# Attention scores as three float32r products, and a shared last step of values for two pairs of heads

## The chip, the cores and the metric

The kernel runs on one core of a Trainium2 chip. The metric is the time of one execution on the device, in microseconds. Engines are named TensorE (PE, with its weight loads as PEld), ScalarE (ACT), VectorE (DVE), GpSimd (POOL) and SyncE (SP, which issues the transfers).

## The reference

Sigmoid attention over 4 batches, 12 heads, 448 tokens and 64 dimensions, then two layers of a feed-forward block on 1792 tokens, all of it in float32:

```python
scores = scale * np.matmul(q, k.transpose(0, 1, 3, 2)) - np.log(S)
attn = 1.0 / (1.0 + np.exp(-scores))
x = np.matmul(attn, v)            # then tokens by 768 columns
h = x @ w_in;  x = (np.maximum(h, 0) ** 2) @ w_out
h = x @ w_in2; out = (np.maximum(h, 0) + alpha * np.minimum(h, 0)) @ w_out2
```

The feed-forward weights come as float64.

## The kernel before

Two stages follow one another. The attention stage works through 24 units; a unit is one batch and two heads. The feed-forward stage then takes the rest of the time; the change leaves its code as it is. All instructions stand in the queues in the order in which the program writes them: TensorE, ScalarE, VectorE, GpSimd and SyncE each work through their own queue.

A unit's 448 keys are 3 x 128 and 64 left over (R = 3, MAIN = 384, REM = 64). Its steps:

- fetch(u), L122: eight transfers on SyncE: q and k for two heads (L135), their last 64 rows (L137), v (L132) and its last 64 rows into vrem (L137). NAT = 3 buffers of each.
- turn(u), L139: seven transposes on TensorE bring q and k to 64 dimensions on the partitions, one head in partitions 0 to 63, the other in 64 to 127, into two accumulator banks; VectorE copies the 896 columns to qkt (L150).
- scores(u, j), L152: for step j of four, the keys of that step (128 columns of weights) against all 448 queries, for each head in its half of the rows (L159), in float32, which gives two matmul instructions for a product; then one sigmoid on ScalarE over both heads, 2 x 448 columns (L161). Two buffers of two banks. In the last step the weights are the 64 left keys and 64 others, so half of the sigmoid's output is not used.
- values(u, j), L164: the step's sigmoids against v, in float32, each head into its half of the columns of one bank (L172), added over the four steps. In the last step the spare 64 rows of vrem are zero (cleared once at the start, L188).
- finish(u), L176, after the last step: the bank goes to the feed-forward stage's x in two parts, a high part in float32r by ScalarE (L184) and the rest by VectorE (L185). The 448 tokens of a batch fall into one tile of x (batch 0) or two (batches 1 to 3; 64 + 384, 128 + 320, 64 + 384 columns), and each piece has its own pair of instructions.

The loop (L193) writes for unit u: scores(u, 0) and (u, 1); values(u-1, 2) and (u-1, 3) with the finish of u-1; fetch(u+2); turn(u+1); scores(u, 2) and (u, 3); values(u, 0) and (u, 1). Weights for the next stage are fetched beside it: load (L62) brings 768 KB through three buffers, assemble (L74) turns float64 into float32 with one instruction on ScalarE (L82) and three on VectorE (L83 to L85), split (L87) makes the high part on ScalarE (L95) and the rest on GpSimd (L96), and then issues the load for three items later, which needs the buffer that GpSimd has just read. Loads 0 to 2 are issued in units 2, 4, 6; assemble(i) stands in unit 8 + 2i, split(i) in unit 9 + 2i, for i from 0 to 5.

In the feed-forward stage each product is three float32r products, high by high, high by low and low by high (L227, L260).

Of the kernel before, what the change touches and what calls it, by code (L numbers as in the profile page):

```python
# [9 lines left out]
F32 = mybir.dt.float32  # L10
F32R = mybir.dt.float32r
I32 = mybir.dt.int32
I64 = mybir.dt.int64
AF = mybir.ActivationFunctionType
ALU = mybir.AluOpType
P = 128
# [3 lines left out]
def fused_kernel(ctx: ExitStack, tc: tile.TileContext, q, k, v, w1i, w1o, w2i, w2o, alpha, out):  # L20
# [12 lines left out]
    nc = tc.nc  # L33
    B, H, S, D = q.shape
# [4 lines left out]
    R = S // P  # L39
    MAIN = R * P  # L40
    REM = S - MAIN
# [3 lines left out]
    SCALE = 1.0 / math.sqrt(D)  # L45
# [9 lines left out]
    bias = const.tile([P, 1], F32, name="bias")  # L55
# [6 lines left out]
    def load(i):  # L62
        if i >= len(items):
            return
        layer, inward, f = items[i]
        w = ((w1i, w1o), (w2i, w2o))[layer][0 if inward else 1]
        raws[i] = wpool.tile([P, DM, 2], I32, tag="raw", name=f"raw{i}", bufs=3)
        d = raws[i].rearrange("p m t -> p (m t)").bitcast(I64)
        if inward:
            nc.sync.dma_start(out=d.rearrange("p (c f) -> p c f", c=NC), in_=w[:, f * P:(f + 1) * P].rearrange("(c p) f -> p c f", p=P))  # L70
        else:
            nc.sync.dma_start(out=d, in_=w[f * P:(f + 1) * P, :])

    def assemble(i):  # L74

        if i >= len(items):
            return  # L80
        low, high = raws[i][:, :, 0], raws[i][:, :, 1]
        nc.scalar.activation(high.bitcast(F32), high.bitcast(F32), AF.Copy, scale=2.0 ** -112)  # L82
        nc.vector.tensor_scalar(out=low, in0=low, scalar1=29, scalar2=None, op0=ALU.logical_shift_right)  # L83
        nc.vector.scalar_tensor_tensor(out=low, in0=high, scalar=3, in1=low, op0=ALU.logical_shift_left, op1=ALU.bitwise_or)  # L84
        nc.vector.scalar_tensor_tensor(out=low, in0=high, scalar=-2 ** 31, in1=low, op0=ALU.bitwise_and, op1=ALU.bitwise_or)  # L85

    def split(i):  # L87
        if i >= len(items):
            return
        layer, inward, f = items[i]  # L90
        w = raws.pop(i)[:, :, 0].bitcast(F32)
        tag = "wi" if inward else "wo"
        hi = wpool.tile([P, DM], F32R, tag=tag + "h", name=f"wh{i}", bufs=3)
        lo = wpool.tile([P, DM], F32R, tag=tag + "l", name=f"wl{i}", bufs=3)
        nc.scalar.activation(hi, w, AF.Copy)  # L95
        nc.gpsimd.tensor_sub(lo, w, hi)  # L96
        ready[items[i]] = (hi, lo)
        load(i + 3)
# [4 lines left out]
    def x_tiles(layer, t, c):  # L103
        n = TILES[t][1]
        if (layer, t, c) not in x:
            x[layer, t, c] = tuple(xpool.tile([P, n], F32R, tag=f"x{part}{t}", name=f"x{part}{layer}_{t}_{c}", bufs=NC) for part in "hl")
        return x[layer, t, c]

    with tc.manual_schedule():
# [6 lines left out]
        with tc.tile_pool(name="apool", bufs=1) as apool, tc.tile_pool(name="apsum", bufs=1, space=bass.MemoryType.PSUM) as psum:  # L116
            units = [(b, c) for b in range(B) for c in range(H // 2)]
            NAT = 3
            nats, qks, vals, qkt, sig, avs = {}, {}, {}, {}, {}, {}
            vrem = [apool.tile([P, 2, D], F32, name=f"vrem{i}") for i in range(NAT)]  # L120

            def fetch(u):  # L122
                if u >= len(units):
                    return
                b, c = units[u]
                hs = slice(2 * c, 2 * c + 2)
                nats[u] = apool.tile([P, 2, R, 2, D], F32, tag="nat", name=f"nat{u}", bufs=NAT)
                vals[u] = apool.tile([P, 2, R, D], F32, tag="v", name=f"v{u}", bufs=NAT)
                qks[u] = apool.tile([P, 2, D], F32, tag="qk", name=f"qk{u}", bufs=NAT)
                for j, src in enumerate((q, k, v)):  # L130
                    if j == 2:
                        nc.sync.dma_start(out=vals[u], in_=src[b, hs, :MAIN, :].rearrange("h (p r) d -> p h r d", r=R))  # L132
                    else:
                        for h in range(2):
                            nc.sync.dma_start(out=nats[u][:, j, :, h, :], in_=src[b, 2 * c + h, :MAIN, :].rearrange("(p r) d -> p r d", r=R))  # L135
                    last = (qks[u][:REM], qks[u][REM:], vrem[u % NAT][:REM])[j]
                    nc.sync.dma_start(out=last, in_=src[b, hs, MAIN:, :].rearrange("h p d -> p h d"))  # L137

            def turn(u):  # L139

                if u >= len(units):
                    return
                ps = psum.tile([P, 1024], F32, tag="tp", name=f"tp{u}", bufs=1)
                for r in range(R):
                    nc.tensor.transpose(ps[:, r * P:(r + 1) * P], nats[u][:, 0, r].rearrange("p h d -> p (h d)"), eye)  # L145
                nc.tensor.transpose(ps[:, MAIN:MAIN + P], qks.pop(u).rearrange("p h d -> p (h d)"), eye)  # L146
                for r in range(R):
                    nc.tensor.transpose(ps[:, 512 + r * P:512 + (r + 1) * P], nats[u][:, 1, r].rearrange("p h d -> p (h d)"), eye)  # L148
                qkt[u] = apool.tile([P, 2 * S], F32, tag="qkt", name=f"qkt{u}", bufs=2)
                nc.vector.tensor_copy(qkt[u], ps[:, :2 * S])  # L150

            def scores(u, j):  # L152

                t = qkt[u]
                at = S if j == R else 512 + j * P
                ps = psum.tile([P, 2, 512], F32, tag="sc", name=f"sc{u}_{j}", bufs=2)
                for h in range(2):
                    rows = slice(h * D, (h + 1) * D)
                    nc.tensor.matmul(ps[:, h, :S], t[rows, at:at + P], t[rows, :S], start=True, stop=True)  # L159
                a = apool.tile([P, 2, S], F32, tag="a", name=f"a{u}_{j}", bufs=6)  # L160
                nc.scalar.activation(a, ps[:, :, :S], AF.Sigmoid, bias=bias, scale=SCALE)  # L161
                sig[u, j] = a

            def values(u, j):  # L164
                if u < 0:
                    return
                if j == 0:
                    avs[u] = psum.tile([P, 512], F32, tag="av", name=f"av{u}", bufs=2)
                a = sig.pop((u, j))
                for h in range(2):  # L170
                    w = vrem[u % NAT][:, h, :] if j == R else vals[u][:, h, j, :]
                    nc.tensor.matmul(avs[u][h * D:(h + 1) * D, :S], w, a[:, h, :], start=(j == 0), stop=(j == R))  # L172
                if j == R:
                    finish(u)

            def finish(u):  # L176
                b, c = units[u]
                ps = avs.pop(u)
                for t, (first, n) in enumerate(TILES):
                    lo, hi = max(first, b * S), min(first + n, (b + 1) * S)  # L180
                    if lo < hi:
                        xh, xl = (p[:, lo - first:hi - first] for p in x_tiles(0, t, c))
                        part = ps[:, lo - b * S:hi - b * S]
                        nc.scalar.activation(xh, part, AF.Copy)  # L184
                        nc.vector.tensor_sub(xl, part, xh)  # L185

            for i in range(NAT):
                nc.gpsimd.memset(vrem[i][REM:], 0.0)  # L188
            fetch(0)
            fetch(1)  # L190
            nc.sync.dma_start(out=al, in_=alpha.rearrange("(f p) -> p f", p=P))
            turn(0)
            for u in range(len(units)):  # L193
                scores(u, 0)
                scores(u, 1)
                values(u - 1, 2)
                values(u - 1, R)
                fetch(u + 2)
                turn(u + 1)
                scores(u, 2)  # L200
                scores(u, R)
                values(u, 0)
                values(u, 1)

                if u in (2, 4, 6):
                    load(u // 2 - 1)
                if u >= 8 and u % 2 == 0 and u // 2 - 4 < 6:
                    assemble(u // 2 - 4)
                if u >= 8 and u % 2 == 1 and u // 2 - 4 < 6:
                    split(u // 2 - 4)  # L210
            values(len(units) - 1, 2)
            values(len(units) - 1, R)


        gpool = ctx.enter_context(tc.tile_pool(name="gpool", bufs=1, reuse_waits="tile"))
# [127 lines left out]
```

## Time and profile before

| | us |
|---|---|
| median of 3 runs | 1135.44 (1134.73 to 1136.49) |
| the profiled execution | 1135.57 |
| its span, first to last instruction | 1133.8 |
| TensorE busy | 1115.6 (98%) |
| VectorE busy | 642.5 (57%) |
| ScalarE busy | 362.2 (32%) |
| first matmul of the feed-forward stage | at 193.53 |

The shares are means over both stages. The attention stage is a sixth of the span. In the views, a time such as 121.38 is in us from the start of the span; a matmul's duration holds its way through the array, so consecutive matmuls overlap, and the distance of their starts tells what one costs.

### The profile page before, as it was taken

How to read it: one execution, taken by the hardware profiler on the slowest of the kernel's cores; microseconds unless marked ns; L12 is line 12 of the kernel's file. 1: busy time of each engine (PE TensorE's matmuls, PEld its weight loads, DVE VectorE, ACT ScalarE, POOL GpSimd, SP SyncE). 2: the span in 40 equal slices, each digit the busy share in tenths (PEclk: the TensorE clock that was granted, in tenths of full speed). 3: DMA queues.
4: the chain of work that ended last, by engine and by line, in shares of the span. 5: the costliest groups of instructions: out<-in, count | busy, mean ns of one | idle time of the engine just before them, and what ended most of it. 6: DMA issues, size and time to landing. Idle time of an engine off the chain costs nothing.

```text
span 1133.8 us, 14165 instructions
## 1 busy us (share of the span) xinstructions
PE 1115.6 (98%) x5736; PEld 933.6 (82%) x5736; DVE 642.5 (57%) x943; ACT 362.2 (32%) x536; POOL 153.2 (14%) x97
## 2 busy tenths in 40 slices
PE   7999999999999999999999999999999999999998
PEld 3444344898989898989898999898989898989998
DVE  1233431335666665656666674567676767767554
ACT  4567765443222222322224543312121212121110
POOL 0001110011111111110103560101010202011000
PEclk9999999999999999999999999999999999999999
DMA  5645551011121202020202020202020211110014
GB/s 110 154 113 140 145 139 39 1 56 56 44 68 32 80 29 84 28 84 29 84 28 84 28 84 29 84 27 80 8 84 28 80 33 56 57 56 28 1 56 139
DMA packets 89265, 73.28 MB, mean 65 GB/s; under 512 B 52592, under 2 KB 83312, under 8 KB 89200
## 3 DMA queue, kind: packets, MB, share of 16 engines
q1 hardware_dynamic: 89200, 72.38, 22.2%
q8 instruction: 45, 0.74, 0.3%
q14 instruction: 20, 0.16, 0.0%
HBM read 66.85 MB, written 5.51 MB: 64 GB/s over the span
## 4 chain that ended last, share of the span: by engine, by line
PE 93%; DVE 4%; ACT 2%; SPq 0%; issue 0%; DMA 0%; ACTq 0%
PE h L227 39%; PE o L260 38%; PE sc L159 7%; PE av L172 7%; DVE raw L84 1%; PE tp L145 1%; PE tp L148 1%; DVE r L237 1%; DVE g L238 1%; ACT gh L239 1%; DVE raw L85 1%; ACT raw L82 1%; ACT wh L95 0%; DVE acc L265 0%; DVE gl L240 0%; PE tp L146 0%
## 5 line engine op out<-in xcount | busy, mean ns | idle before, releaser
L227 PE MATMUL h<-xh,wl 128*128 128x512 f32 (+1 forms) x768 | 278.5, 363 | 0.0
L227 PE MATMUL h<-xl,wh 128*128 128x512 f32 (+1 forms) x768 | 278.3, 362 | 0.0
L227 PE MATMUL h<-xh,wh 128*128 128x512 f32 (+1 forms) x768 | 277.9, 362 | 0.0
L96 POOL TENSOR_TENSOR wl<-raw,wh 128x768 fp32r<-128x768 f32 x64 | 122.3, 1911 | 908.1 <-ACT wh L95 850.6
L265 DVE TENSOR_TENSOR acc<-o,acc 128x384 f32<-128x384 f32 (+1 forms) x364 | 200.0, 584 | 76.8 <-PE o L260 75.3
L260 PE MATMUL o<-wh,gh 128*128 128x384 f32 x448 | 150.6, 336 | 6.5 <-DVE acc L265 6.2
L227 PEld LDWEIGHTS h<-xh,wh 128*128 128x128 f32 x768 | 144.2, 188 | 15.6 <-issue 0.7
L227 PEld LDWEIGHTS h<-xl,wh 128*128 128x128 f32 x768 | 144.1, 188 | 15.1
L227 PEld LDWEIGHTS h<-xh,wl 128*128 128x128 f32 x768 | 144.1, 188 | 15.1
L260 PE MATMUL o<-wl,gh 128*128 128x384 f32 x448 | 149.9, 335 | 0.0
L260 PE MATMUL o<-wh,gl 128*128 128x384 f32 x448 | 149.8, 334 | 0.0
L260 PE MATMUL o<-gh,wl 128*128 128x512 f32 (+1 forms) x384 | 139.1, 362 | 0.0
L260 PE MATMUL o<-gl,wh 128*128 128x512 f32 (+1 forms) x384 | 139.0, 362 | 0.0
L260 PE MATMUL o<-gh,wh 128*128 128x512 f32 (+1 forms) x384 | 138.9, 362 | 0.0
L239 ACT ACTIVATE gh<-g 128x512 fp32r<-128x512 f32 (+1 forms) x64 | 37.1, 579 | 284.4 <-DVE g L238 284.4
L240 DVE TENSOR_TENSOR gl<-g,gh 128x512 fp32r<-128x512 f32 (+1 forms) x128 | 93.0, 727 | 52.3 <-ACT gh L239 45.4
L95 ACT ACTIVATE wh<-raw 128x768 fp32r<-128x768 f32 x64 | 57.3, 896 | 175.1 <-DVE raw L85 129.2
L161 ACT ACTIVATE a<-sc,bias 128x896 f32<-128x896 f32 x96 | 91.8, 1005 | 57.4 <-PE sc L159 57.4
L234 DVE SCALAR_TENSOR_TENSOR g<-h,r 128x512 f32<-128x512 f32 (+1 forms) x64 | 39.9, 623 | 113.9 <-ACT r L233 113.9
L84 DVE SCALAR_TENSOR_TENSOR raw<-raw 128x768 int32<-128x768 int32 x64 | 81.1, 1267 | 39.6 <-ACT raw L82 35.4
L233 ACT ACTIVATE r<-h 128x512 f32<-128x512 f32 (+1 forms) x64 | 34.8, 544 | 186.4 <-PE h L227 185.7
L260 PEld LDWEIGHTS o<-wh,gh 128*128 128x128 f32 x448 | 84.1, 188 | 9.4 <-DVE acc L265 8.1
(39 smaller groups left out, 1094.6 us busy)
## 6 DMA issues: line engine op xcount, KB each, us to landing
raw<-in_moe_w_in_dram SPq DMA_DIRECT2D x32, 768.0 KB, 4.8
raw<-in_moe_w_out_dram SPq DMA_DIRECT2D x32, 768.0 KB, 4.3
nat<-in_q_dram SPq DMA_DIRECT2D x48, 96.0 KB, 2.9
nat<-in_k_dram SPq DMA_DIRECT2D x48, 96.0 KB, 2.9
v<-in_v_dram SPq DMA_DIRECT2D x24, 192.0 KB, 2.7
out_dram<-acc SPq DMA_DIRECT2D x16, 192.0 KB, 2.7
out_dram<-acc SPq DMA_DIRECT2D x6, 384.0 KB, 2.3
qk<-in_q_dram SPq DMA_DIRECT2D x24, 32.0 KB, 2.5
```

The costliest lines, as they stand in the source:

```text
L84: nc.vector.scalar_tensor_tensor(out=low, in0=high, scalar=3, in1=low, op0=ALU.logical_shift_left, op1=ALU.bitwise_or)
L95: nc.scalar.activation(hi, w, AF.Copy)
L96: nc.gpsimd.tensor_sub(lo, w, hi)
L159: nc.tensor.matmul(ps[:, h, :S], t[rows, at:at + P], t[rows, :S], start=True, stop=True)
L161: nc.scalar.activation(a, ps[:, :, :S], AF.Sigmoid, bias=bias, scale=SCALE)
L172: nc.tensor.matmul(avs[u][h * D:(h + 1) * D, :S], w, a[:, h, :], start=(j == 0), stop=(j == R))
L227: nc.tensor.matmul(ps[:, :n], wp[:, c * P:(c + 1) * P], xp, start=(c == 0 and i == 0), stop=(c == NC - 1 and i == 2))
L234: nc.vector.scalar_tensor_tensor(out=gt, in0=ps[:, :n], scalar=0.0, in1=r, op0=ALU.max, op1=ALU.mult)
L239: nc.scalar.activation(gh, gt, AF.Copy)
L240: nc.vector.tensor_sub(gl, gt, gh)
L260: nc.tensor.matmul(ps[:, :size], *ops, start=(i == 0), stop=(i == len(turns) - 1))
L265: nc.vector.tensor_add(part, ps[:, :size], part)
```

## The change

- turn makes two tiles of q and k in float32r instead of one in float32: a high part, by VectorE's copy, and a low part, by a VectorE subtraction from the same accumulators.
- scores makes three float32r products per head and step (high by high, high by low, low by high), added in the accumulators, where one float32 product stood.
- The last 64 keys of a unit go to partitions 0 to 63 for even units and 64 to 127 for odd ones (the 128 columns of weights begin 64 earlier for these), and the sigmoid takes these 64 partitions alone, into a tile that the two units of a pair share. The last 64 rows of v are laid out in the same way.
- The last step of values is done for both units of a pair at one place, last_values: four products of 64 rows by 64 columns. Both finishes follow there.
- The loop goes over pairs of units (u, w = u + 1). It has the same steps; values(u, 3) is gone from the middle, fetch(u+3) and turn(u+2) stand after values(u, 2). assemble(i) and split(i-1) both stand at the end of a pair's steps, so that each split, and the load behind it, comes one unit later.
- v has four buffers, and the clearing of vrem is gone.

```diff
--- before.py
+++ after.py
@@ -116,8 +116,7 @@
         with tc.tile_pool(name="apool", bufs=1) as apool, tc.tile_pool(name="apsum", bufs=1, space=bass.MemoryType.PSUM) as psum:
             units = [(b, c) for b in range(B) for c in range(H // 2)]
             NAT = 3
-            nats, qks, vals, qkt, sig, avs = {}, {}, {}, {}, {}, {}
-            vrem = [apool.tile([P, 2, D], F32, name=f"vrem{i}") for i in range(NAT)]
+            nats, qks, vals, vrems, parts, sig, avs = {}, {}, {}, {}, {}, {}, {}
 
             def fetch(u):
                 if u >= len(units):
@@ -125,16 +124,21 @@
                 b, c = units[u]
                 hs = slice(2 * c, 2 * c + 2)
                 nats[u] = apool.tile([P, 2, R, 2, D], F32, tag="nat", name=f"nat{u}", bufs=NAT)
-                vals[u] = apool.tile([P, 2, R, D], F32, tag="v", name=f"v{u}", bufs=NAT)
+                vals[u] = apool.tile([P, 2, R, D], F32, tag="v", name=f"v{u}", bufs=NAT + 1)
                 qks[u] = apool.tile([P, 2, D], F32, tag="qk", name=f"qk{u}", bufs=NAT)
+                if u % 2 == 0:
+                    vrems[u // 2] = apool.tile([P, 2, D], F32, tag="vrem", name=f"vrem{u}", bufs=3)
                 for j, src in enumerate((q, k, v)):
                     if j == 2:
                         nc.sync.dma_start(out=vals[u], in_=src[b, hs, :MAIN, :].rearrange("h (p r) d -> p h r d", r=R))
                     else:
                         for h in range(2):
                             nc.sync.dma_start(out=nats[u][:, j, :, h, :], in_=src[b, 2 * c + h, :MAIN, :].rearrange("(p r) d -> p r d", r=R))
-                    last = (qks[u][:REM], qks[u][REM:], vrem[u % NAT][:REM])[j]
+                    last = (qks[u][:REM], qks[u][REM:], vrems[u // 2][half(u)])[j]
                     nc.sync.dma_start(out=last, in_=src[b, hs, MAIN:, :].rearrange("h p d -> p h d"))
+
+            def half(u):
+                return slice(u % 2 * REM, (u % 2 + 1) * REM)
 
             def turn(u):
 
@@ -146,32 +150,48 @@
                 nc.tensor.transpose(ps[:, MAIN:MAIN + P], qks.pop(u).rearrange("p h d -> p (h d)"), eye)
                 for r in range(R):
                     nc.tensor.transpose(ps[:, 512 + r * P:512 + (r + 1) * P], nats[u][:, 1, r].rearrange("p h d -> p (h d)"), eye)
-                qkt[u] = apool.tile([P, 2 * S], F32, tag="qkt", name=f"qkt{u}", bufs=2)
-                nc.vector.tensor_copy(qkt[u], ps[:, :2 * S])
+                parts[u] = [apool.tile([P, 2 * S], F32R, tag=f"qk{part}", name=f"qk{part}{u}", bufs=2) for part in "hl"]
+                nc.vector.tensor_copy(parts[u][0], ps[:, :2 * S])
+                nc.vector.tensor_sub(parts[u][1], ps[:, :2 * S], parts[u][0])
 
             def scores(u, j):
 
-                t = qkt[u]
-                at = S if j == R else 512 + j * P
+                hi, lo = parts[u]
+                at = 512 + j * P if j < R else S - u % 2 * REM
                 ps = psum.tile([P, 2, 512], F32, tag="sc", name=f"sc{u}_{j}", bufs=2)
-                for h in range(2):
-                    rows = slice(h * D, (h + 1) * D)
-                    nc.tensor.matmul(ps[:, h, :S], t[rows, at:at + P], t[rows, :S], start=True, stop=True)
-                a = apool.tile([P, 2, S], F32, tag="a", name=f"a{u}_{j}", bufs=6)
-                nc.scalar.activation(a, ps[:, :, :S], AF.Sigmoid, bias=bias, scale=SCALE)
-                sig[u, j] = a
+                for i, (kt, qt) in enumerate(((hi, hi), (hi, lo), (lo, hi))):
+                    for h in range(2):
+                        rows = slice(h * D, (h + 1) * D)
+                        nc.tensor.matmul(ps[:, h, :S], kt[rows, at:at + P], qt[rows, :S], start=(i == 0), stop=(i == 2))
+                if j < R:
+                    a = sig[u, j] = apool.tile([P, 2, S], F32, tag="a", name=f"a{u}_{j}", bufs=6)
+                    at = slice(0, P)
+                else:
+                    if u % 2 == 0:
+                        sig[u // 2] = apool.tile([P, 2, S], F32, tag="ar", name=f"ar{u}", bufs=2)
+                    a = sig[u // 2]
+                    at = half(u)
+                nc.scalar.activation(a[at], ps[at, :, :S], AF.Sigmoid, bias=bias[at], scale=SCALE)
 
             def values(u, j):
                 if u < 0:
                     return
                 if j == 0:
                     avs[u] = psum.tile([P, 512], F32, tag="av", name=f"av{u}", bufs=2)
-                a = sig.pop((u, j))
+                a, w = sig.pop((u, j)), vals[u]
                 for h in range(2):
-                    w = vrem[u % NAT][:, h, :] if j == R else vals[u][:, h, j, :]
-                    nc.tensor.matmul(avs[u][h * D:(h + 1) * D, :S], w, a[:, h, :], start=(j == 0), stop=(j == R))
-                if j == R:
-                    finish(u)
+                    nc.tensor.matmul(avs[u][h * D:(h + 1) * D, :S], w[:, h, j, :], a[:, h, :], start=(j == 0), stop=False)
+
+            def last_values(d):
+
+                if d < 0:
+                    return
+                a, w = sig.pop(d), vrems.pop(d)
+                for h in range(2):
+                    for u in (2 * d, 2 * d + 1):
+                        nc.tensor.matmul(avs[u][h * D:(h + 1) * D, :S], w[half(u), h, :], a[half(u), h, :], start=False, stop=True)
+                finish(2 * d)
+                finish(2 * d + 1)
 
             def finish(u):
                 b, c = units[u]
@@ -184,32 +204,41 @@
                         nc.scalar.activation(xh, part, AF.Copy)
                         nc.vector.tensor_sub(xl, part, xh)
 
-            for i in range(NAT):
-                nc.gpsimd.memset(vrem[i][REM:], 0.0)
             fetch(0)
             fetch(1)
             nc.sync.dma_start(out=al, in_=alpha.rearrange("(f p) -> p f", p=P))
             turn(0)
-            for u in range(len(units)):
+            for u in range(0, len(units), 2):
+                w = u + 1
                 scores(u, 0)
                 scores(u, 1)
                 values(u - 1, 2)
-                values(u - 1, R)
+                last_values(u // 2 - 1)
                 fetch(u + 2)
-                turn(u + 1)
+                turn(w)
                 scores(u, 2)
                 scores(u, R)
                 values(u, 0)
                 values(u, 1)
-
+                scores(w, 0)
+                scores(w, 1)
+                values(u, 2)
+                fetch(u + 3)
+                turn(u + 2)
+                scores(w, 2)
+                scores(w, R)
+                values(w, 0)
+                values(w, 1)
+
+                i = u // 2 - 4
                 if u in (2, 4, 6):
                     load(u // 2 - 1)
-                if u >= 8 and u % 2 == 0 and u // 2 - 4 < 6:
-                    assemble(u // 2 - 4)
-                if u >= 8 and u % 2 == 1 and u // 2 - 4 < 6:
-                    split(u // 2 - 4)
+                if 0 <= i < 6:
+                    assemble(i)
+                if 0 < i < 7:
+                    split(i - 1)
             values(len(units) - 1, 2)
-            values(len(units) - 1, R)
+            last_values(len(units) // 2 - 1)
 
 
         gpool = ctx.enter_context(tc.tile_pool(name="gpool", bufs=1, reuse_waits="tile"))
```

## Rows read from the trace of the kernel before

**Rows 1.** The table of stretches, 120 to 150 us.

```profile
core 0: us, PE busy (x) PEld busy (x) DVE busy (x) ACT busy (x) POOL busy (x), PEclk, DMA share, GB/s
120.00:150.00 30.00, 30.00 (x156) 12.37 (x156) 11.90 (x18) 21.07 (x28) 3.70 (x2) 1.00 0.59 145
```

**Rows 2.** The chain in order of time, one unit: start us, us, what.

```profile
120.06 0.48 PE tp L145 x3
...
120.97 1.70 PE sc L159 x8
122.68 1.65 PE av L172 x8
...
127.69 0.48 PE tp L145 x3
128.17 0.11 PE tp L146
128.28 0.33 PE tp L148 x3
```

**Rows 3.** The timeline of TensorE, a group of scores: start us, us, engine line operation.

```profile
120.90 0.30 PEld L159 LDWEIGHTS sc<-qkt 64*128 64x128 f32 x4 [0.17 <-issue]
121.38 0.54 PE L159 MATMUL sc<-qkt 64*128 64x448 f32 x2
121.39 0.19 PEld L159 LDWEIGHTS sc<-qkt 64*128 64x128 f32 x2 [0.18 <-ACT xh L184]
121.76 0.54 PE L159 MATMUL sc<-qkt 64*128 64x448 f32 x2
```

**Rows 4.** The timeline of TensorE in the feed-forward stage, float32r products.

```profile
302.74 0.33 PE L260 MATMUL o<-gh,wl 128*128 128x384 f32 x1
302.92 0.39 PE L227 MATMUL h<-xh,wh 128*128 128x512 f32 x1
303.15 0.40 PE L227 MATMUL h<-xl,wh 128*128 128x512 f32 x1
```

**Rows 5.** The timeline of TensorE at the end of the attention stage.

```profile
190.37 2.48 PE L172 MATMUL av<-a,v 128*64 128x448 f32 x12
...
193.53 0.50 PE L227 MATMUL h<-xh,wh 128*128 128x512 f32 x1
```

**Rows 6.** The timeline of ScalarE and VectorE, one finish and what follows.

```profile
120.11 0.28 ACT L184 ACTIVATE xh<-av 128x128 fp32r<-128x128 f32 x1 [0.44 <-PE av L172]
120.42 0.29 DVE L185 TENSOR_TENSOR xl<-av,xh 128x128 fp32r<-128x128 f32 x1 [5.34 <-ACT xh L184]
120.74 0.44 ACT L184 ACTIVATE xh<-av 128x320 fp32r<-128x320 f32 x1 [0.36 <-DVE xl L185]
121.21 0.49 DVE L185 TENSOR_TENSOR xl<-av,xh 128x320 fp32r<-128x320 f32 x1 [0.50 <-ACT xh L184]
121.62 1.08 DVE L150 COPY qkt<-tp 128x896 f32<-128x896 f32 x1
122.03 1.91 ACT L161 ACTIVATE a<-sc,bias 128x896 f32<-128x896 f32 x2 [0.86 <-PE sc L159]
```

**Rows 7.** Groups by line and shape, 0 to 215 us: busy, mean ns | idle before.

```profile
L185 DVE TENSOR_TENSOR xl<-av,xh 128x448 fp32r<-128x448 f32 x6 | 3.8, 625 | 36.5 <-ACT xh L184 36.5
L184 ACT ACTIVATE xh<-av 128x448 fp32r<-128x448 f32 x6 | 3.3, 543 | 2.7 <-PE av L172 2.7
```

**Rows 8.** The timeline around a split and the load behind it (SPq: SyncE).

```profile
116.20 0.91 ACT L95 ACTIVATE wh<-raw 128x768 fp32r<-128x768 f32 x1
116.63 1.77 PE L159 MATMUL sc<-qkt 64*128 64x448 f32 x8
117.18 1.85 POOL L96 TENSOR_TENSOR wl<-raw,wh 128x768 fp32r<-128x768 f32 x1 [13.42 <-ACT wh L95]
119.06 0.35 SPq L72 DMA_DIRECT2D raw<-in_moe_w_out_dram  x1
...
123.43 0.62 SPq L137 DMA_DIRECT2D qk<-in_k_dram  x1
```

**Rows 9.** The view of line 137, 103 to 175 us: its transfers.

```profile
DMA to landing us min/median/max: 2.2/2.6/4.7
```

## The prediction

> **What bounds the kernel now.** I read the table of stretches first: from 120 to 150 us, in the middle of the attention stage, TensorE is busy all the time at a granted clock of 1.00 (2.4 GHz), ScalarE 70% and VectorE 40% [rows 1]. Then the chain in order of time for one unit (two heads) of that stage: it is TensorE alone, 7.63 us from one turn to the next (127.69 - 120.06), made of a turn of 0.92 (0.48 + 0.11 + 0.33), two groups of scores of 1.70 and two groups of values of 1.65 [rows 2]. The change touches this stage only, so what counts is how many microseconds of TensorE a unit needs, and whether another engine becomes late. The loads of weights and the matmuls one by one show the inside of a group: loads come two at a time, and so do the matmuls, whose pairs start 0.38 apart (121.38, 121.76) [rows 3]. A pair is one half of the work of a float32 product for both heads, side by side in the two row halves (a float32 product is two matmul instructions here). So a step of scores is two pairs, 0.75, a group of two steps 1.50, and 0.20 of its 1.70 is the change from one shape to the next. For values it is 0.15 of 1.65.
>
> **Scores in three products.** Per step two float32 pairs go, and three float32r pairs come. The trace has no float32r product in row halves. The nearest rows are the full-height float32r products of the later stage: 0.18 from start to start at 384 columns, 0.23 at 512 [rows 4]; 448 lies between, and I take 0.20. Two halves of 64 rows that run side by side would keep this pitch, as the float32 halves do; one after the other they would need 0.40. I take 0.20, since a float32 pair shows the halves side by side in this very place, and keep 0.40 as the far end. A group of two steps is then 6 x 0.20 + 0.20 = 1.40 in place of 1.70: 0.30 saved, four times in two units.
>
> A load of weights seems to cost nothing: it starts with the matmul pair in front of it, in the same two halves (121.39), and the next pair starts 0.38 later, which is a pair's own time all through the group [rows 2, 3]. The Trainium skill says otherwise (TensorE: Matmul & The Clock Gate, "Part 3: Packing small matmuls — row/col tiling"): a load overlaps matmuls in flight only when it goes to another row group. By that rule each of the three pairs would also pay its load; the trace here does not agree with it, but shows it for float32 only.
>
> **Last 64 keys shared.** Before, each unit spends one step of values, 0.75, on keys of which half are zeros. After, two units spend one step together, if the four 64x64 quarters run at once; the trace shows two column halves at once (8 matmuls of values in 1.65) and two row halves at once [rows 2, 3], never four quarters. I take 0.75 for all four, and as the far end two at a time, 1.50. The quarters are a shape of their own, so I give them a change of shape, 0.15, as for a lone group: 0.90.
>
> **Two units of TensorE time** (u even, w = u + 1), in the order of the new loop: scores(u) A 1.40; values(u-1, 2) and the shared step B 0.90 + 0.90; turn(w) C 0.92; scores(u) D 1.40; values(u) E 1.65; scores(w) F 1.40; values(u, 2) G 0.90; turn(u+2) H 0.92; scores(w) I 1.40; values(w) J 1.65. Sum 13.44, against 2 x 7.63 = 15.26: 1.82 less, 21.8 us for the 12 pairs. At the end, J and B come before the next stage, 3.45, where before it is 190.37 to 193.53, 3.16 [rows 5]: 0.3 back.
>
> **What comes late instead.** VectorE now makes two parts per unit: the copy (1.08 [rows 6]) and a subtraction of 896 columns from the accumulators. Subtractions of 320 and 448 columns take 0.49 and 0.63 [rows 6, 7], about 1.05 ns per column, so 1.10 for 896. And both units of a pair finish at the same place, ahead of this copy in VectorE's queue. Count from the start of A. B ends at 3.20; the first ScalarE copy starts 0.05 after the values end (120.06, 120.11) [rows 2, 6], at 3.25. One finish in two parts goes ScalarE, VectorE, ScalarE, VectorE, each waiting for the other, and takes 1.59 (120.11 to 121.70) [rows 6]: 4.84. The second unit's first ScalarE copy ran meanwhile, but its VectorE part is next: 0.29, then ScalarE 0.44, VectorE 0.49, with gaps of 0.03: 6.15. Copy to 7.25, subtraction to 8.36, and some 0.05 until TensorE sees it: 8.4. TensorE reaches F at 7.17, does its first pair (high by high) and wants the low part at about 7.4. So it waits 1.0 in F. Behind that wait everything on TensorE is queued: the rest of F, then G, H. Where a unit falls into one part of the output (the first batch, three pairs) the finish is 0.54 on ScalarE and twice 0.63 on VectorE [rows 7]: 3.25 + 0.54 + 1.30 + 2.2 = 7.3, just in time. Eight pairs pay 1.0: 8.0 us. The lone turn in H has VectorE free: its parts are there 2.2 later, and I and J cover 3.05.
>
> ScalarE: per pair the same 8 sigmoids (two take 1.91 [rows 6], however many partitions they have) and 4 to 8 copies, so some 11 of 14 us. The weights' copies, 0.91 each [rows 8], now come two in a row, after sigmoid (w, R), which ends 0.4 ahead of A (the copy starts at 116.20, the scores at 116.63). They hold sigmoid (u, 0) to 1.4 and the second to 3.3, and the first finish with it: 0.1 in five pairs, 0.5 in all.
>
> SyncE: the split, and the load behind it, move one unit later, and that load waits for GpSimd. Ahead of it now lie two ScalarE copies (to 1.4) and 1.85 on GpSimd [rows 8]: issue at 3.3 (before, too, it follows GpSimd's end at once: 117.18 + 1.85, 119.06). Queued behind it on SyncE is fetch(u+2). Its last part for k is issued 4.4 after the load (123.43) and lands 2.6 later in the median, 4.7 at most [rows 9]: 10.3. H wants it at 7.17 + 1.40 + 1.0 + 0.90 + 0.33 = 10.8. It is in time only because F has waited, so these two costs do not add; a slow landing costs up to 2 once or twice, which the range holds. The clearing of the spare rows at the start goes too, 3 memsets beside the first transfers, worth nothing.
>
> Sum against the profiled execution (1135.57 us, with a span of 1133.8; the median of the runs is 1135.44): -21.8 + 0.3 + 8.0 + 0.5 = -13.0, so 1122.6.
>
> **The rivals.**
> (a) No wait in F: VectorE or ScalarE orders the finishes better than I count, for instance if the second unit's parts need not alternate. The 0.36 gap at 120.74 speaks against it [rows 6]. Then 8.5 comes back, but the load holds H for about 0.6 in five pairs: 1114 to 1117.
> (b) The quarters run two at a time: 0.75 x 12 = 9 more, 1131.6. Nothing in the trace shows four.
> (c) A load of weights is not hidden in float32r, the two halves' loads 0.11 each at the least (0.30 for two pairs of loads against 0.19 for one [rows 3]). Then a pair takes 0.31: 24 x 0.11 = 2.64 more per pair of units, 31.7, less 6.2 because the wait in F shrinks by seven pitches (0.77) in eight pairs: 1148.1. This is what the rule of the Trainium skill's page TensorE: Matmul & The Clock Gate would do here.
> (d) The other side: the row halves of float32r do not run side by side. The place is the score groups, the price 24 x 0.20 x 12 = 57.6, less the 8.5 that vanish: 1171.7. The float32 pairs speak against it. The point from which this and (c) decide: each 0.01 on the pitch costs 2.9 without and 2.3 with the wait's shrinking, so the 13.0 are gone at a pitch of about 0.255.
> (e) The step does not do what it says: the shared quarters and the new shape cost what they save (1.5 to 1.6 for B's second part) and the pitch is 0.23: 1122.6 + 9 + 7 = 1138.6, no gain that could be told.
>
> **How the numbers follow.** Forecast 1122.6 (1119 to 1126): 0.55. (a) 0.12, (b) and smaller misses of the pitch up to 0.23: 0.17, (c) 0.04, (d) 0.07, (e) 0.05. The range leaves out (c), (d) and (e): 1113.5 to 1132.5. A measurement here can tell 0.2%, 2.3 us: faster holds the forecast, (a) and (b), 0.84; no difference 0.05; slower 0.11.
>
> **What would show it.** In the trace of after: score groups of 1.40 with pairs 0.20 apart; four matmuls of 64x64 with starts together, twice, 0.38 apart; a wait of about 1 us on TensorE for VectorE's subtraction at the first scores of odd units, absent in the first pairs; the later stages unchanged, starting near 181 in place of 193.5. I am wrong if score pairs stand 0.3 or more apart, if the 64x64 matmuls come in four starts, or if TensorE waits longest for transfers.

## The result and the profile after

| | before | after |
|---|---|---|
| median, us | 1135.97 (1134.73 to 1136.49, 4 runs) | 1126.38 (1125.93 to 1126.66, 4 runs) |
| the profiled execution, us | 1135.57 | 1126.52 |
| its span, us | 1133.8 | 1124.7 |
| first matmul of the feed-forward stage | at 193.53 | at 184.49 |

The ratio is 0.9917, with a 95% interval of 0.99 to 0.9934: faster, by 9.6 us or 0.8%, where 13.0 were forecast (1122.6). All of it is in the attention stage: its end moved by 9.04, the whole execution by 9.05.

The chain in order of time, in one of the first pairs of units (start us, us, what), answers to [rows 2]:

```profile
27.38 0.48 PE tp L149 x3
...
28.30 1.42 PE sc L165 x12
29.71 1.65 PE av L183 x8
31.37 1.41 PE sc L165 x11
32.78 0.90 PE av L183 x4
33.68 0.48 PE tp L149 x3
...
39.08 0.90 PE av L183 x4
39.98 0.91 PE av L192 x8
40.89 0.48 PE tp L149 x3
```

It is TensorE alone: a group of scores takes 1.41 where it took 1.70, the lone step of values 0.90, the shared step 0.91, and the pair 13.51 (40.89 - 27.38), against 15.26. The first three pairs that finish units go like this. From the fourth on there are waits. TensorE in such a pair (the timeline, start us, us, line, operation, idle time before and what ended it):

```profile
126.65 0.56 PE L192 MATMUL av<-ar,vrem 64*64 64x448 f32 x4
...
128.05 0.47 PE L165 MATMUL sc<-qkh 64*128 64x448 f32 x2
128.36 0.36 PE L165 MATMUL sc<-qkl,qkh 64*128 64x448 f32 x2
128.56 0.37 PE L165 MATMUL sc<-qkh,qkl 64*128 64x448 f32 x2
...
131.85 0.47 PE L165 MATMUL sc<-qkh 64*128 64x448 f32 x2 [0.51 <-DVE qkh L154]
132.89 0.47 PE L165 MATMUL sc<-qkl,qkh 64*128 64x448 f32 x2 [0.57 <-DVE qkl L155]
```

The pairs of float32r products stand 0.31 apart at the head of a group and 0.20 behind it. Each quarter is two matmul instructions, and the eight of a shared step start in two fours, at 126.22 and 126.65 (the row above is the second four, its starts 7 ns apart). At the first scores of the odd unit TensorE waits for both of VectorE's parts, the high one and then the low one. The waits of TensorE over the stage (us in total, times, longest):

```profile
PE sc L165 <- DVE qkl L155: 4.9, 9, 0.6
...
PE sc L165 <- DVE qkh L154: 3.8, 6, 1.2
```

These count idle time after the last modelled end of a matmul, so they are less than what a pair loses. From shared step to shared step the pairs take 13.51, 13.53, 13.51, then 14.47 and 14.49, then five times 15.08 to 15.21, and 11.99 for the last (which has no turn in its second half). The chain behind a long one:

```profile
123.86 0.91 ACT raw L82
...
124.80 0.97 DVE raw L84
...
125.79 2.53 DVE raw L85
128.32 0.21 DVE xl L205
...
130.71 1.01 DVE qkh L154
...
131.74 1.10 DVE qkl L155
...
132.89 1.29 PE sc L165 x10
```

VectorE's last assembling step, L85, stands ahead of the finishes and takes 2.53. In the kernel before it takes 0.96 (attention stage: busy, mean ns | idle before):

```profile
L85 DVE SCALAR_TENSOR_TENSOR raw<-raw 128x768 int32<-128x768 int32 x6 | 5.8, 963 | 0.2
```

The timeline of GpSimd and VectorE at this place, after:

```profile
124.80 0.96 DVE L84 SCALAR_TENSOR_TENSOR raw<-raw 128x768 int32<-128x768 int32 x1 [1.15 <-ACT raw L82]
125.65 1.85 POOL L96 TENSOR_TENSOR wl<-raw,wh 128x768 fp32r<-128x768 f32 x1 [13.25 <-DMA v<-in_v_dram]
125.79 2.53 DVE L85 SCALAR_TENSOR_TENSOR raw<-raw 128x768 int32<-128x768 int32 x1
```

The new loop has put the split of one weight tile directly behind the assembling of the next, and GpSimd's subtraction runs beside L85. L84, which began ahead of the subtraction, kept its 0.96; L85, which began 0.14 behind it, did not.

### The profile page after: what moved, and what is told of

It is laid out like the page before. It is cut to its first block, busy times and chain, and to the rows that moved or that the text cites. A ratio compares the mean times of both kernels' runs of the same rounds, so it can differ in the third digit from the quotient of the medians.

```text
span 1124.7 us, 14542 instructions
## 1 busy us (share of the span) xinstructions
PE 1098.4 (98%) x5928; PEld 948.1 (84%) x5928; DVE 676.2 (60%) x967; ACT 361.3 (32%) x536; POOL 152.6 (14%) x94
## 4 chain that ended last, share of the span: by engine, by line
PE 87%; DVE 8%; ACT 4%; issue 1%; SPq 0%; DMA 0%; ACTq 0%
PE h L256 39%; PE o L289 38%; PE sc L165 4%; PE av L183 3%; DVE raw L85 2%; DVE raw L84 2%; DVE xl L205 1%; ACT raw L82 1%; DVE qkl L155 1%; DVE qkh L154 1%; ACT xh L204 1%; DVE r L266 1%; DVE g L267 1%; PE tp L149 1%; ACT gh L268 1%; PE av L192 1%
## 5 line engine op out<-in xcount | busy, mean ns | idle before, releaser
L84 DVE SCALAR_TENSOR_TENSOR raw<-raw 128x768 int32<-128x768 int32 x64 | 81.0, 1266 | 36.2 <-ACT raw L82 32.3
L174 ACT ACTIVATE a<-sc,bias 128x896 f32<-128x896 f32 x72 | 70.0, 1005 | 51.9 <-PE sc L165 51.5
```

The source lines that it names most:

```text
L174: nc.scalar.activation(a[at], ps[at, :, :S], AF.Sigmoid, bias=bias[at], scale=SCALE)
```

## Experiments

Theory A: the waits come from the order of VectorE's queue (the finishes of two units ahead of the next unit's two parts), and in five pairs L85, slowed beside GpSimd, adds to it. Rivals: ScalarE's copies or the load hold these pairs (B); VectorE simply has too much work (C); a transfer takes the wait's place (D). Times of the runs stand beside the kernel before on the same chip (1134.8 to 1135.0).

**The split half a pair earlier.**

```diff
                 turn(u + 2)
+                i = u // 2 - 4
+                if 0 < i < 7:
+                    split(i - 1)
                 scores(w, 2)
...
                 if 0 <= i < 6:
                     assemble(i)
-                if 0 < i < 7:
-                    split(i - 1)
```

> The changed kernel with one edit: the split of a weight tile stands after turn(u+2), half a pair earlier, so that GpSimd's subtraction no longer runs beside the last VectorE step of the next tile's assembling (L85). Theory A: the five pairs that take 15.1 us do so because that step takes 2.53 in place of 0.96 beside GpSimd, and the finishes behind it start 0.65 later. Then L85 is back at 0.96, the five pairs take 14.5, and the time is 1126.4 - 5 x 0.65 = 1123.2. Rival B: ScalarE's copies of the weights, ahead of the sigmoids, or the load that waits for GpSimd hold these pairs. The copies stay as many, so the pairs stay at 15.1 or move by 0.2 at most, and the time stays at 1126 (1125.4 to 1126.8).

Measured: 1122.33 us (1122.01 to 1123.0), ratio 0.9889 (0.9874 to 0.9904). The seven long pairs all take 14.41 to 14.47 now, and the last stays at 11.99. L85 over the stage (busy, mean ns | idle before), first in the changed kernel:

```profile
L85 DVE SCALAR_TENSOR_TENSOR raw<-raw 128x768 int32<-128x768 int32 x6 | 13.6, 2267 | 0.2
```

and in this run:

```profile
L85 DVE SCALAR_TENSOR_TENSOR raw<-raw 128x768 int32<-128x768 int32 x6 | 5.8, 960 | 0.2
```

GpSimd's subtraction now runs beside other VectorE work:

```profile
118.86 1.09 DVE L154 CAST qkh<-tp 128x896 fp32r<-128x896 f32 x1 [3.19 <-PE tp L152]
...
119.27 1.87 POOL L96 TENSOR_TENSOR wl<-raw,wh 128x768 fp32r<-128x768 f32 x1 [12.55 <-ACT wh L95]
...
119.98 1.09 DVE L155 TENSOR_TENSOR qkl<-tp,qkh 128x896 fp32r<-128x896 f32 x1
```

The copy and the subtraction that read the accumulators keep their 1.09 beside it. So 4 us hang on where the split stands, and it matters which VectorE step runs beside it. The edit also moves one of ScalarE's copies out of the way, so it does not yet part A from B.

**VectorE's assembling steps one place later**, all else where it is.

```diff
-    def assemble(i):
+    def assemble(i, part=0):
...
-        nc.scalar.activation(high.bitcast(F32), high.bitcast(F32), AF.Copy, scale=2.0 ** -112)
+        if part != 2:
+            nc.scalar.activation(high.bitcast(F32), high.bitcast(F32), AF.Copy, scale=2.0 ** -112)
+        if part == 1:
+            return
...
                 turn(w)
+                if 0 < u // 2 - 4 < 7:
+                    assemble(u // 2 - 5, 2)
...
-                    assemble(i)
+                    assemble(i, 1)
```

> The changed kernel with the split where it is, and ScalarE's two copies where they are; only VectorE's three assembling steps (L83 to L85) stand one place later, behind turn(w) of the next pair, when GpSimd's subtraction is over and the finishes are through. Theory A: L85 takes 0.96 again and nothing of it stands ahead of the finishes; what is left in the five pairs is ScalarE's part alone, the first finish at 3.5 after the pair's start in place of 3.25, a wait of 1.2 in place of 1.0, 14.7 per pair: 1126.4 - 5 x 0.4 = 1124.4. Rival B (ScalarE's copies or the load hold these pairs, not VectorE): 15.1 per pair and 1126.4.

Measured: 1124.8 us (1124.02 to 1125.39), ratio 0.9912 (0.9895 to 0.9928). ScalarE's copies still stand two in a row, but four of the five pairs take 14.53 to 14.74; the other takes 15.62, of which the profile puts a wait of 0.9 down to a transfer of k. So the copies cost about 0.1 a pair (14.53 to 14.58 in three pairs, against 14.41 to 14.47 in the run before), and VectorE's slowed step, ahead of the finishes, the other 0.5 to 0.6. B falls.

**The split ahead of the assembling**, at the same place.

```diff
-                if 0 <= i < 6:
-                    assemble(i)
                 if 0 < i < 7:
                     split(i - 1)
+                if 0 <= i < 6:
+                    assemble(i)
```

> The changed kernel with the split written ahead of the next tile's assembling, at the same place: the same instructions, ScalarE's two copies in the other order, so that GpSimd starts 0.9 earlier and ends about 2.4 after the pair's start. Theory A (VectorE's steps are slowed only while GpSimd's subtraction runs): L85 is back at 0.96, L84 takes about 1.9, the finishes start some 0.35 late instead of 0.9, and the five pairs take about 14.8: 1126.4 - 5 x 0.3 = 1124.9. Rival B (ScalarE's two copies hold the pairs): the same two copies stand at the same place, 15.1 per pair and 1126.4.

Measured: 1127.08 us (1126.43 to 1127.51), ratio 0.9929 (0.9912 to 0.9946), the five pairs 15.28 to 15.41.

```profile
124.44 1.87 POOL L96 TENSOR_TENSOR wl<-raw,wh 128x768 fp32r<-128x768 f32 x1 [13.42 <-ACT wh L95]
...
125.21 1.91 DVE L84 SCALAR_TENSOR_TENSOR raw<-raw 128x768 int32<-128x768 int32 x1 [1.98 <-ACT raw L82]
...
127.16 0.96 DVE L85 SCALAR_TENSOR_TENSOR raw<-raw 128x768 int32<-128x768 int32 x1
```

The slowing moved from L85 to L84, as theory A has it, and L85 is back at 0.96. The time was missed by 2.2: I had forgotten that the other copy, which L84 needs, now comes 0.8 later, so that L85 ends at 128.12, 4.6 after the pair's first scores (123.50), where the changed kernel has 128.32 and 4.4 (123.89). The time alone would have spoken for B; the rows do not: beside GpSimd it is now L84 that is slow.

**The second finish behind scores(u, 3).**

```diff
                 finish(2 * d)
-                finish(2 * d + 1)
+                if d == len(units) // 2 - 1:
+                    finish(2 * d + 1)
...
                 scores(u, 2)
                 scores(u, R)
+                if u:
+                    finish(u - 1)
```

> The changed kernel with one edit: of the two finishes of a pair the second stands after scores(u, 3), so that VectorE makes the next unit's two parts ahead of it. Theory A: the wait in the first scores of odd units comes from the order of VectorE's queue, two finishes of 1.6 and 1.3 ahead of copy and subtraction of 2.2. Then the three pairs of 14.5 go to 13.5, and of the five pairs of 15.1 some 0.45 stays, since L85 still ends late: 1126.4 - 3 x 1.0 - 5 x 1.15 = 1117.6. Rival C: the wait is VectorE's bare work (two parts per unit, 2.2, where there was one copy) or ScalarE's, and only moves when the order changes: the time stays within 2 of 1126.4.

Measured: 1119.8 us (1119.34 to 1121.09), ratio 0.9865 (0.9848 to 0.9881). The two pairs of 14.47 and 14.49 go to 13.53 and 13.51, and the last from 11.99 to 11.04: the wait is the order of VectorE's queue, with the same steps in it, and C falls. The five others take 14.14 to 15.50, 2.2 more in sum over the run than expected. TensorE's waits:

```profile
PE tp L150 <- DMA qk<-in_k_dram: 4.0, 4, 1.6
...
PE sc L165 <- DVE qkl L155: 0.4, 1, 0.4
```

Of the waits for VectorE in the pairs none is left (the 0.4 is at the start); the waits for the last 64 rows of k are new but for 1.6 at the start. The load waits for GpSimd, the fetch waits behind the load, and what hid it was the wait in the scores.

**Both edits together.**

> Both edits together: the split half a pair earlier, and the second finish of a pair behind scores(u, 3). Theory A: VectorE then has the low part ready before the first scores of every odd unit, the load goes out some 3 us earlier so that no transfer is late either, and every pair takes the 13.52 that the pairs without a wait show: 1126.4 - 3 x 0.97 - 5 x 1.6 = 1115.5. Rival D: with the wait gone another one takes its place (the transfers of the next unit, as in the run with the second finish late, up to 1.6 us in a turn): 1118 or more.

Measured: 1115.33 us (1114.76 to 1115.5), ratio 0.9824 (0.981 to 0.9839), the fastest of all. Every pair takes 13.51 to 13.53, and the last 11.05. The table of stretches (us, busy of PE, PEld, DVE, ACT, POOL, then clock, share and GB/s of the transfers) from 120 to 150 us, first the changed kernel, then this one:

```profile
120.00:150.00 30.00, 27.69 (x188) 14.70 (x188) 19.25 (x22) 20.88 (x29) 3.71 (x2) 1.00 0.59 144
```

```profile
120.00:150.00 30.00, 30.00 (x211) 15.94 (x211) 18.12 (x26) 23.45 (x32) 3.74 (x2) 1.00 0.67 169
```

TensorE is busy all the time again, as in [rows 1], and no transfer is late, since the load now goes out half a pair earlier. D falls for this order.

**The scores alone**, in the loop of before.

```diff
-                qkt[u] = apool.tile([P, 2 * S], F32, tag="qkt", name=f"qkt{u}", bufs=2)
-                nc.vector.tensor_copy(qkt[u], ps[:, :2 * S])
+                parts[u] = [apool.tile([P, 2 * S], F32R, tag=f"qk{part}", name=f"qk{part}{u}", bufs=2) for part in "hl"]
+                nc.vector.tensor_copy(parts[u][0], ps[:, :2 * S])
+                nc.vector.tensor_sub(parts[u][1], ps[:, :2 * S], parts[u][0])
...
-                for h in range(2):
-                    rows = slice(h * D, (h + 1) * D)
-                    nc.tensor.matmul(ps[:, h, :S], t[rows, at:at + P], t[rows, :S], start=True, stop=True)
+                for i, (kt, qt) in enumerate(((hi, hi), (hi, lo), (lo, hi))):
+                    for h in range(2):
+                        rows = slice(h * D, (h + 1) * D)
+                        nc.tensor.matmul(ps[:, h, :S], kt[rows, at:at + P], qt[rows, :S], start=(i == 0), stop=(i == 2))
```

> The kernel before, with the score part of the change alone: two parts per unit and three float32r products in row halves; the last 64 keys, the loop and the place of the splits as before. Theory A: a group of scores costs 1.41 in place of 1.70, 48 groups, 13.9 in all, and one finish per unit leaves VectorE time for both parts (they end at about 6.9 of a unit's 7.0, in time). So 1135.6 - 13.9 = 1121.7, faster than the whole change. Rival C (two parts per unit are too much for VectorE whatever stands ahead of them): each unit waits some 0.5 to 1, and the time is 1133 or more.

Measured: 1122.83 us (1122.09 to 1123.67), ratio 0.9893 (0.9878 to 0.9908): 12.2 of the 13.9 counted, and 3.5 us better than the whole change.

**The shared last step alone**, with float32 scores in the new loop.

```diff
-                parts[u] = [apool.tile([P, 2 * S], F32R, tag=f"qk{part}", name=f"qk{part}{u}", bufs=2) for part in "hl"]
-                nc.vector.tensor_copy(parts[u][0], ps[:, :2 * S])
-                nc.vector.tensor_sub(parts[u][1], ps[:, :2 * S], parts[u][0])
+                qkt[u] = apool.tile([P, 2 * S], F32, tag="qkt", name=f"qkt{u}", bufs=2)
+                nc.vector.tensor_copy(qkt[u], ps[:, :2 * S])
...
-                for i, (kt, qt) in enumerate(((hi, hi), (hi, lo), (lo, hi))):
-                    for h in range(2):
-                        rows = slice(h * D, (h + 1) * D)
-                        nc.tensor.matmul(ps[:, h, :S], kt[rows, at:at + P], qt[rows, :S], start=(i == 0), stop=(i == 2))
+                for h in range(2):
+                    rows = slice(h * D, (h + 1) * D)
+                    nc.tensor.matmul(ps[:, h, :S], t[rows, at:at + P], t[rows, :S], start=True, stop=True)
```

> The changed kernel with float32 scores again (one part, one copy per unit, one product): the shared last step, the new loop and the place of the splits alone. Theory A: a pair of units has 5.98 of values in place of 6.60, 0.6 less, 7.5 in all; VectorE has one step of 1.08 after the finishes, done at 7.3 of the 7.8 that TensorE leaves it, and only in the five pairs with the slowed L85 some 0.1 to 0.3 late. So 1135.6 - 7.5 + 1 = 1129. Rival C' (the two finishes in one place are late by themselves): a wait of 0.5 or more in eight pairs, 1132 or more.

Measured: 1129.45 us (1128.87 to 1129.88), ratio 0.9951 (0.9936 to 0.9966). L85 takes 2.53 here too, but no scores wait more than 0.09 for VectorE; the one new wait that the profile lists is for a transfer of k, 0.54. Alone the two parts give 12.2 and 5.5; together, as changed, 9.6, and with the order mended 19.6.

**The products of one head after those of the other.**

```diff
-                for i, (kt, qt) in enumerate(((hi, hi), (hi, lo), (lo, hi))):
-                    for h in range(2):
+                for h in range(2):
+                    for i, (kt, qt) in enumerate(((hi, hi), (hi, lo), (lo, hi))):
```

> The changed kernel with the three products of one head written together, then those of the other: the same 576 products in another order, so that neighbours in TensorE's queue share a half of the rows. It measures what the alternation of the halves is worth. Theory A (TensorE starts matmuls in the order written, and two run side by side only where neighbours are in different halves): of the six products of a step one pair overlaps within the step and one with the next, a step takes 0.8 in place of 0.6, a group of two some 1.9 in place of 1.41, and since the waits for VectorE shrink, the time is about 1140 (1135 to 1146). Rival E (no overlap at all this way): a group takes 2.6 and the time is about 1172. Rival F (TensorE brings the halves together by itself): 1126.

Measured: 1128.13 us (1127.85 to 1128.93), ratio 0.9939 (0.9924 to 0.9954), 1.8 above the changed kernel. A group that waits for nothing:

```profile
124.54 0.47 PE L165 MATMUL sc<-qkh 64*128 64x448 f32 x2
124.84 0.36 PE L165 MATMUL sc<-qkl,qkh 64*128 64x448 f32 x2
125.04 0.37 PE L165 MATMUL sc<-qkh,qkl 64*128 64x448 f32 x2
...
125.95 0.97 PE L183 MATMUL av<-a,v 128*64 128x448 f32 x4
```

Both heads still start together, product by product, though three products of one head now stand ahead of the first of the other, and the group takes 1.41 (124.54 to 125.95). Rival F holds here, and my expectation missed. A group that waits for VectorE shows where this ends:

```profile
132.52 0.44 PE L165 MATMUL sc<-qkh 64*128 64x448 f32 x1 [0.51 <-DVE qkh L154]
133.55 0.47 PE L165 MATMUL sc<-qkl,qkh 64*128 64x448 f32 x1 [0.59 <-DVE qkl L155]
133.56 0.47 PE L165 MATMUL sc<-qkh 64*128 64x448 f32 x1
133.86 0.36 PE L165 MATMUL sc<-qkh,qkl 64*128 64x448 f32 x1
```

The second head's first product (133.56) needs the high part alone, which was there at 132.52. Yet it starts only behind the first head's second product (133.55), which stands ahead of it in the queue and waits for the low part; and it starts ahead of the first head's third (133.86). So a product that waits for another engine holds up all that stand behind it, and products that need not wait pass each other between the halves. One pair of products less is done before the wait, one pitch of 0.20: these groups take 2.46 in place of 2.25, eight times, which is most of the 1.8.

## Why the prediction was right or wrong

The time lay in the range, and the way it went and most of its mechanism were as forecast; the gain was 3.4 us smaller by the medians, 3.9 by the profiled executions (1126.5 against 1122.6).

- Scores: a group of 1.40 was forecast, 1.41 to 1.42 came. The float32r halves run side by side, which [rows 3] showed for float32 alone, and the pitch of 0.20 read between [rows 4] holds. The load of weights is hidden in float32r too, so rivals (c) and (d) are out, and so is the rule of the Trainium skill (TensorE: Matmul & The Clock Gate, "Part 3: Packing small matmuls — row/col tiling") that a load overlaps only matmuls of another row group: with the 0.31 of rival (c) a group would take about 2.1. (The same section also lets a load go ahead into the background buffer of weights, which this does not speak against.)
- Quarters: all four at once, 0.91 against 0.90. Rival (b) is out.
- The pair: 13.52 against 13.44, 1.0 in twelve pairs.
- The wait in the scores of odd units: 1.0 was forecast in eight pairs, none in the first three. The first three show none; the three without the slowed step show 0.95 (14.47 and 14.49 against 13.52, and 11.99 against the 11.04 of the run without a wait). The run with the second finish late confirms its cause.
- The five pairs with a split: here the step failed. I gave them 0.1 each for ScalarE's copies; they take 15.08 to 15.21, some 0.65 over the 14.48 of the others, 3.3 in all. ScalarE's part was sized right (0.1, by the run with the steps later), though its copies begin at the pair's start (123.86, the scores at 123.89) and not 0.4 ahead. The missing term is VectorE's: I counted the finishes from the moment ScalarE could start them and left out what stands ahead of them in VectorE's queue, L84 and L85, and that L85 would run beside GpSimd. The trace of before had it. In the attention stage the three assembling steps never meet GpSimd's subtraction; in the feed-forward stage they do, and the means over the whole program tell it (first 0 to 215 us, then all):

```profile
L84 DVE SCALAR_TENSOR_TENSOR raw<-raw 128x768 int32<-128x768 int32 x6 | 5.8, 960 | 9.7 <-ACT raw L82 9.7
L83 DVE TENSOR_SCALAR raw<-raw 128x768 int32<-128x768 int32 x6 | 3.3, 552 | 0.0
```

```profile
L84 DVE SCALAR_TENSOR_TENSOR raw<-raw 128x768 int32<-128x768 int32 x64 | 81.1, 1267 | 39.6 <-ACT raw L82 35.4 <-DVE raw L83 0.5
L83 DVE TENSOR_SCALAR raw<-raw 128x768 int32<-128x768 int32 x64 | 53.4, 834 | 0.0
```

  One by one: 19 of the 64 L84 began while a GpSimd subtraction ran. They take 1.70 to 2.10, the others 0.96, and each of the 19 ends 0.81 to 0.83 after that subtraction, as if nearly all of its work came behind it. For L83 the end is 0.42 after it (13 times, up to 2.11 in place of 0.55), while the 15 that began ahead of the subtraction kept 0.55. The 28 additions from the accumulators (L265) that ran beside one keep their time. L85 in the changed kernel ends at 128.32, 0.82 after GpSimd's 127.50, which is what the trace of before gives.

  The Trainium skill states it too (SBUF — State Buffer, "Who interferes with whom"): a VectorE instruction with two inputs from SBUF contends with a GpSimd instruction that reads SBUF, for ports that one of them holds alone, while one with at most one SBUF input does not, outside the modes that use two ports. The rows agree for L84 and L85 (two SBUF inputs) and for the steps that read the accumulators. L83 has a single SBUF input and is held up all the same; no row here shows in which mode it goes.
- The load: forecast as in time only because the scores wait, with some 0.6 in five pairs otherwise (rival (a)). With the wait taken away and the load left, the turns of five pairs lost 0.2 to 1.6, 3.4 in all.
- The rest, 0.5, is the start: the second group of scores, from 13.89 on, takes 2.23, where it took 1.96 before and should have taken some 0.3 less. Its products stand 0.37 apart until 15.55, nearly twice the later 0.20; before, the later distance holds from 14.55 on. The granted clock reads 1.00 all through, and why the slow start lasts longer stays open.

So 1122.6 + 1.0 (pairs) - 0.4 (wait) + 2.8 (slowed step, less the 0.5 counted) + 0.5 (start) = 1126.5. Rival (a)'s time, 1114 to 1117, is what the two edits together reach, by another order of the queues and not by the one in the change.

## What to carry to other kernels

When two finishes are gathered at one place, walk through the in-order queue of the engine behind them, with everything that stands ahead in it, and ask what the next stage waits for; here the order alone was worth 10 to 11 us (9.6 and 19.6 gained). When a step is moved, list what will run beside it on the other engines, and look in the trace for the same step with and without that neighbour: two means for one shape are the sign. A wait that vanishes uncovers the next one, so move the load that stood behind it as well.

## What the runs showed of the hardware

- A VectorE step on two SBUF inputs went from 0.96 to 2.53 (L85) or 1.91 (L84) beside a GpSimd subtraction of 1.85 that had begun ahead of it, and ended 0.81 to 0.82 after it; L84 that began first kept 0.96, and steps that read the accumulators stayed at 1.09.
- Four float32 quarters of 64x64 run at once, 0.91 for the step with its change of shape.
- A sigmoid over 896 columns takes 1.00 on 64 partitions and 1.01 on 128 (means of 24 and 72 in the changed kernel).
- TensorE started products of the second head ahead of products of the first that stand before them in its queue: the records show pairs 0.01 apart where the written order has three of one head first. The Trainium skill (TensorE: Matmul & The Clock Gate, "Part 3: Packing small matmuls — row/col tiling") says that matmuls start and end in program order; the records here do not agree with it for matmuls in different row halves. It is not only how the profile dates them: with 0.20 between two products of one half, starts in the written order would make a group take about 1.9 (an estimate from this pitch, as in the expectation), and it takes 1.41. A product that waits for VectorE still holds up those behind it, of either half.
